# Routed experts: three more parts of rows do their second layer with the rows moving, and the buffer for turned results is doubled

## The chip, the cores and the metric

One core of a Trainium2 chip runs the whole kernel as one program. TensorE (PE, with PEld for its loading of the stationary operand), VectorE (DVE), ScalarE (ACT), GpSimd (POOL) and SyncE (SP) each work through their own list of instructions and wait for each other by semaphores. The metric is the device time in microseconds (us); the median of three runs counts.

## The reference, cut to what matters

```
# x: (8, 1856, 256) -> rfft over 1856, complex 256x256 layer, soft threshold, irfft -> 14848 rows of 256
for each row:  group g = argmax(x @ w_group), expert e = argmax(x @ w_expert[g]), weight = g_w * e_w
for each of the 16 experts:  h = relu(rows @ w1[e])     # 256 -> 1024, the first layer
                             out[rows] = weight * (h @ w2[e])   # 1024 -> 256, the second layer
```

Each row goes to one expert. The sizes of the experts' groups of rows depend on the data, so the kernel sorts rows into lists in memory and works through fixed portions of these lists; a loop at the end takes what is left over.

## The kernel before, in words

**Two stages.** The first 440 us or so are the transform, the routing, and early portions of four experts, in an order written out by hand (the string ORDER). The change leaves this stage alone. Then comes the loop over **parts** (`for i, (kind, q) in enumerate(jobs)`): 40 parts of 256 to 432 rows, each of one expert. Their rows are, in the order of the work (part 0 first):

```
0-3    256 304 432 400        15-17  256 384 336       27-29  256 384 256
4-6    384 384 336            18-20  256 384 288       30-32  256 320 256
7-8    256 256                21-23  256 384 288       33-35  256 320 256
9-11   384 384 320            24-26  256 384 256       36-37  416 384
12-14  384 384 288                                     38-39  320 384
```

**A step.** Step i of the loop issues, in this order on every engine: the second layer of part i-1 (wholly or in part), the first layer of part i, the preparing of the rows of part i+1, and what was left of the second layer of part i-1. The order of instructions on each engine is the order of this code; no scheduler moves them.

**First layer** (`up_g`). The hidden units come in 8 blocks of 128. For a block TensorE runs 6 matmuls with the part's rows moving (line 619; values are split into a high and a low half, so three products per half of the 256 inputs). ScalarE then takes the block out of PSUM with a ReLU (line 624, high half `hh`), and VectorE makes the low half `hl` (line 627). Between the blocks other work is issued: after odd blocks a piece of `back_g` (below), after even blocks a piece of `deal_g`, which gathers rows for part i+2 by indirect DMA on POOL (line 560) and passes them on by SP (line 572). In steps where weights of a coming expert arrive, 8 pieces of weight splitting stand between the blocks as well (line 524 on ScalarE, 525 on VectorE).

**Second layer, plain** (`down_g`). For each tile of up to 128 rows: 16 matmuls, the rows' hidden values as the stationary operand and 512 or 256 columns of weights moving (lines 695 and 696). A last tile of 48 or 80 rows has the same 16 matmuls. ScalarE and VectorE each take out one half (lines 700 and 701), and POOL stores the tile's rows in the output by an indirect DMA (line 669). Two tiles are done before the first layer of part i, the remaining tiles after it.

**Second layer, turned** (`turned_g`, `back_g`). 48 matmuls with the weights stationary and all rows of the part moving (line 717), all before the first layer of part i. The result has the 256 outputs on the partitions, in two halves; ScalarE and VectorE copy one each into the tile `yt` (line 719). In the *next* step, inside the first layer of part i+1, TensorE turns `yt` back with two transposes for each tile of rows (line 730), two tiles after block 1 and the rest after block 3; ScalarE and VectorE scale them out (lines 738 and 736), and POOL stores them. Nothing is left for after the first layer.

**Which parts are turned** (line 1446): those whose row count is in TURNED and whose predecessor is not turned: parts 1, 3, 11, 14, 20, 23, 31, 34, 36 and 38, ten in all.

Preparing the rows of part i+1 (`turn_rows`, lines 582 to 589) takes VectorE and ScalarE; TensorE needs the result at the next first layer. Where the second layer of part i-1 leaves tiles for after the first layer, these matmuls give ScalarE and VectorE time to take out the last blocks before the second layer of part i reads them.

Of the kernel before, what the change touches and what calls it, by code (L numbers as in the profile page):

```python
# [9 lines left out]
F32 = mybir.dt.float32  # L10
# [27 lines left out]
CUTS = ((384, 384, 336), (384, 384, 320), (384, 384, 288), (256, 384, 336), (256, 384, 288), (256, 384, 288), (256, 384, 256),  # L38
        (256, 384, 256), (256, 320, 256), (256, 320, 256), (416, 384), (320, 384))
FCUTS = ((256, 256), (432,), (400,), (256, 304))  # L40
TURNED = (400, 416, 320, 304, 288)
WIDE = 432
LAM = 0.01

# [92 lines left out]
def spectral_moe(ctx: ExitStack, tc: tile.TileContext, x, wri, bri, wgate, w1, w1q, w2, cst, out):  # L137
# [304 lines left out]
    def drain(gen):  # L442
        for _ in gen:
            pass
# [85 lines left out]
    def emit(todo, n):  # L530
        for _ in range(min(n, len(todo))):
            piece, i, cs = todo.pop(0)
            piece(i, cs)

    def fetch(mp, ids, bufs, rows=NPAD + 1, late=False):
        n = ids.n
        out_ = []
        for c0 in range(0, n, 2):
            w = min(2, n - c0)
            xg = mp.tile([128, 2, D], F32, name="xg", bufs=bufs)  # L540
            for c in range(w):
                m = ids.rows(c0 + c)
                ins = nc.gpsimd.indirect_dma_start(
                    out=xg[0:m, c, :], out_offset=None, in_=ys_d[0:rows, :],
                    in_offset=bass.IndirectOffsetOnAxis(ap=ids.gi[0:m, c0 + c:c0 + c + 1], axis=0))
                if late:
                    behind(ins, "stores of the early jobs go first")
            out_.append((xg, w, ids.rows(c0 + w - 1)))
        return out_
# [109 lines left out]
    def h_tiles():  # L659
        return hq.tile([128, 8, WIDE], F32R, name="hh"), hq.tile([128, 8, WIDE], F32R, name="hl")  # L660
# [15 lines left out]
    def down_g(pp, nm, h2, ids, wt, key, tiles, end=False):  # L676
        hh, hl = h2
        w2b, w2h = wt[2], wt[3]
        for t in tiles:
            m = ids.rows(t)  # L680
            o = pp.tile([128, 512], F32, name=nm)[0:m]
            ts = slice(t * 128, t * 128 + m)
            gate_w = ids.ent[0:m, t, 1:2]
            ysb = yp[-1].tile([128, D], F32, name="yo")[0:m]
            if end and t == ids.n - 1:
                o = o[:, 0:D]
                for f in range(8):
                    for a_, b_ in ((hh, w2h), (hh, w2b[:, 1]), (hl, w2h)):
                        nc.tensor.matmul(o, lhsT=a_[:, f, ts], rhs=b_[:, f, :], start=f == 0 and a_ is hh and b_ is w2h,
                                         stop=f == 7 and a_ is hl)  # L690
                nc.scalar.activation(out=ysb, in_=o, func=AF.Copy, scale=gate_w)
                store(ysb, ids, t, key)
                return
            for f in range(8):
                nc.tensor.matmul(o, lhsT=hh[:, f, ts], rhs=w2b[:, :, f, :], start=f == 0, stop=f == 7, skip_group_check=True)  # L695
                nc.tensor.matmul(o[:, 0:D], lhsT=hl[:, f, ts], rhs=w2h[:, f, :], start=False, stop=f == 7,  # L696
                                 skip_group_check=True)
                if f == 3:
                    yield
            nc.scalar.activation(out=ysb, in_=o[:, D:], func=AF.Copy, scale=gate_w)  # L700
            nc.vector.scalar_tensor_tensor(out=ysb, in0=o[:, 0:D], scalar=gate_w, in1=ysb, op0=ALU.mult, op1=ALU.add)  # L701
            store(ysb, ids, t, key)
            yield

    def down(*args):
        drain(down_g(*args))

    def turned_g(pp, nm, h2, ids, wt, yt):
        hh, hl = h2
        w2b, w2h = wt[2], wt[3]  # L710
        n = ids.rows()
        for dh in range(2):
            o = pp.tile([128, 512], F32, name=nm)[:, 0:n]
            ds_ = slice(dh * 128, dh * 128 + 128)
            for f in range(8):
                for w_, h_ in ((w2h, hh), (w2h, hl), (w2b[:, 1], hh)):
                    nc.tensor.matmul(o, lhsT=w_[:, f, ds_], rhs=h_[:, f, 0:n], start=f == 0 and h_ is hh and w_ is w2h,  # L717
                                     stop=f == 7 and h_ is hh and w_ is not w2h)
            (nc.vector.tensor_copy if dh else nc.scalar.copy)(out=yt[:, dh, 0:n], in_=o)
            yield  # L720

    def back_g(pp, nm, yt, ids, key):
        for t0 in range(0, ids.n, 2):
            o = pp.tile([128, 512], F32, name=nm)
            tiles = range(t0, min(ids.n, t0 + 2))
            for t in tiles:
                m = ids.rows(t)
                for dh in range(2):
                    c = (t - t0) * 256 + dh * 128
                    nc.tensor.transpose(o[0:m, c:c + 128], yt[:, dh, t * 128:t * 128 + m], ident)  # L730
            for t in tiles:
                m, cs = ids.rows(t), slice((t - t0) * 256, (t - t0) * 256 + 256)
                ysb = yp[-1].tile([128, D], F32, name="yo")[0:m]
                gate_w = ids.ent[0:m, t, 1:2]
                if t % 2:
                    nc.vector.tensor_scalar(out=ysb, in0=o[0:m, cs], scalar1=gate_w, scalar2=None, op0=ALU.mult)
                else:
                    nc.scalar.activation(out=ysb, in_=o[0:m, cs], func=AF.Copy, scale=gate_w)
                store(ysb, ids, t, key)
            yield  # L740
# [3 lines left out]
    jobs = [(0, 0), (0, 1), (1, 0), (1, 1), (0, 2), (1, 2), (2, NF), (3, NF)]  # L744
# [417 lines left out]
    xq = ctx.enter_context(tc.tile_pool(name="xq", bufs=2, reuse_waits="tile"))  # L1162
# [253 lines left out]
    def of(k):  # L1416
        return [("r", (k, i)) for i in range(len(CUTS[k]))]

    def fixed(e):
        return [("l", (e, i)) for i in range(len(FCUTS[e]))]  # L1420

    jobs = fixed(3) + fixed(1) + fixed(2) + of(0) + fixed(0)
# [4 lines left out]
    raws, jids, jw, rids, ready = {}, {}, {}, {}, {}  # L1427
# [18 lines left out]
            jids[j] = fids[q[0]][1][q[1]]  # L1446

    def turned(i):
        return 0 < i < len(jobs) - 1 and jids[i].rows() in TURNED and not turned(i - 1)

    prev, behind_, todo, ahead = None, iter(()), [], {}
    DEALT = jobs.index(("r", (0, 0)))
# [6 lines left out]
    for i, (kind, q) in enumerate(jobs):  # L1459
        ids = jids[i]  # L1460
        if kind == "r":
            wt = wts["r", q[0]] = jw[i] if i in jw else wts["r", q[0]]
        else:
            wt = wts[q[0]] = jw[i] if i in jw else wts[q[0]]
        nxt = fetch(xp2, jids[i + 1], 3, late=i == 0) if i + 1 < DEALT else None
        rest, back = iter(()), behind_
        behind_ = iter(())
        if prev is not None:
            pids = prev[1]
            if turned(i - 1):  # L1470
                yt = xq.tile([128, 2, WIDE], F32, name="yt", bufs=1)
                rest = turned_g(psy, "py", prev[0], pids, prev[2], yt)
                drain(rest)
                behind_ = back_g(psy, "py", yt, pids, "out")
            else:
                n2 = min(2, pids.n)
                down(psy, "py", prev[0], pids, prev[2], "out", range(n2))
                rest = down_g(psy, "py", prev[0], pids, prev[2], "out", range(n2, pids.n))
        ready.pop(i, lambda: None)()
        gathers = iter(())  # L1480
        if DEALT <= i + 2 < len(jobs):
            if jobs[i + 2][0] == "r":
                k, part = jobs[i + 2][1]
                jids[i + 2] = rids[k][part]
            ahead[i + 2] = []
            gathers = deal_g(jids[i + 2], ahead[i + 2])
        every = 1 if todo or ids.rows() < 384 else 0
        if i in split_at:
            jw[split_at[i]], todo = split_w(raws.pop(split_at[i]))
        hs = h_tiles()  # L1490
        for f, _ in enumerate(up_g(psh, x2, ids.rows(), wt, hs)):
            if f % 2:
                next(back, None)
            else:
                next(gathers, None)
            if f % 2 or not every:
                emit(todo, 1)
            for _ in range(1 if i else 3):
                next(table, None)
        if i not in split_at or not every:  # L1500
            emit(todo, len(todo))
        if i == 0 or i in split_at:
            dma_next(i)
        if nxt is None and i + 1 < len(jobs):
            x2 = turn_rows(ahead.pop(i + 1).pop(), jids[i + 1])
        drain(gathers)
        drain(rest)
        prev = (hs, ids, wt)
        if nxt is not None:
            x2 = prep(xq, nxt, jids[i + 1].rows())  # L1510
# [66 lines left out]
```

## Time and profile before

| | |
|---|---|
| median of three runs | 1068.2 us (1068.2, 1059.08, 1074.6) |
| the profiled execution | 1074.4 us |
| its span, first to last instruction | 1072.6 us |
| mean granted TensorE clock | 0.986 of full |
| busy share: TensorE, VectorE, ScalarE, POOL | 96%, 69%, 45%, 40% |
| loop over the parts | from 442.6 us to the end |

The profiled execution took 1.8 us more than its span, and lies near the top of the three timed runs. A busy share is an average over both stages. Matmuls overlap, so the time from one matmul's start to the next one's start is what it costs, and the duration in its row is longer than that.

### The profile page before, as it was taken

How to read it: one execution, taken by the hardware profiler on the slowest of the kernel's cores; microseconds unless marked ns; L12 is line 12 of the kernel's file. 1: busy time of each engine (PE TensorE's matmuls, PEld its weight loads, DVE VectorE, ACT ScalarE, POOL GpSimd, SP SyncE). 2: the span in 40 equal slices, each digit the busy share in tenths (PEclk: the TensorE clock that was granted, in tenths of full speed). 3: DMA queues.
4: the chain of work that ended last, by engine and by line, in shares of the span. 5: the costliest groups of instructions: out<-in, count | busy, mean ns of one | idle time of the engine just before them, and what ended most of it. 6: DMA issues, size and time to landing. Idle time of an engine off the chain costs nothing.

```text
span 1072.6 us, 25269 instructions
## 1 busy us (share of the span) xinstructions
PE 1024.9 (96%) x9496; PEld 888.0 (83%) x9496; DVE 742.3 (69%) x1754; ACT 484.4 (45%) x1273; POOL 434.0 (40%) x600
## 2 busy tenths in 40 slices
PE   8999999999999999999999999999999999999996
PEld 4886767776867888889988899979998898999995
DVE  6879999999998665436566665665665656767652
ACT  2664645545636243234344444444544535445532
POOL 0120164465463657633235324334342343443432
PEclk9999999999999999989999999999998999999998
DMA  9402512412314320312342442433424244244210
GB/s 383 146 2 91 187 42 106 152 63 81 121 60 180 122 105 28 126 53 67 126 139 79 142 140 72 137 88 126 146 68 135 62 146 140 70 143 139 79 52 29
DMA packets 63407, 117.25 MB, mean 109 GB/s; under 512 B 20588, under 2 KB 44473, under 8 KB 56754
## 3 DMA queue, kind: packets, MB, share of 16 engines
q1 hardware_dynamic: 46450, 67.81, 19.7%
q0 software_dynamic: 11936, 30.79, 9.0%
q10 hardware_dynamic: 4896, 17.01, 4.1%
q8 instruction: 76, 1.25, 0.5%
q14 instruction: 49, 0.40, 0.1%
HBM read 71.37 MB, written 32.46 MB: 97 GB/s over the span
## 4 chain that ended last, share of the span: by engine, by line
PE 61%; DVE 17%; issue 8%; POOL 4%; DMA 3%; SPq 3%; ACT 2%; another core or an unknown queue 0%; ACTq 0%; POOLq 0%; DVEq 0%
PE ph L619 20%; PE py L695 8%; PE pw L887 5%; PE py L717 5%; PE py L696 4%; SPq L572 3%; PE ph L1047 2%; PE pw L869 2%; PE bank L805 2%; PE bank L911 2%; PE bank L929 2%; DVE big L525 2%; DVE hl L627 2%; PE bank L435 2%; DVE big L439 2%
## 5 line engine op out<-in xcount | busy, mean ns | idle before, releaser
L619 PE MATMUL ph<-xth,big 128*128 128x256 f32 (+8 forms) x1280 | 291.7, 312 | 3.8 <-ACT xth L588 3.0
L627 DVE SCALAR_TENSOR_TENSOR hl<-ph,hh 128x256 fp32r<-128x256 f32 (+8 forms) x528 | 167.6, 355 | 132.6 <-ACT hh L624 78.4
L624 ACT ACTIVATE hh<-ph 128x256 fp32r<-128x256 f32 (+8 forms) x528 | 151.2, 339 | 182.1 <-PE ph L619 134.0
L695 PE MATMUL py<-big,hh 128*128 128x512 f32 (+2 forms) x608 | 222.5, 404 | 1.9 <-ACT hh L624 1.4
L619 PEld LDWEIGHTS ph<-xth,big 128*128 128x128 f32 x1280 | 216.6, 188 | 7.6 <-ACT xth L588 5.0
L619 PE MATMUL ph<-xtl,big 128*128 128x256 f32 (+8 forms) x640 | 199.1, 311 | 2.8 <-DVE xtl L589 2.4
L669 POOL DMA_INDIRECT out_dram<-yo,si_r x92 | 92.6, 1006 | 251.0 <-DVE yo L701 204.7
L696 PE MATMUL py<-big,hl 128*128 128x256 f32 (+2 forms) x608 | 175.5, 289 | 5.2 <-DVE hl L627 4.8
L695 PEld LDWEIGHTS py<-big,hh 128*128 128x128 f32 (+2 forms) x608 | 115.7, 190 | 30.3 <-ACT hh L624 2.3
L560 POOL DMA_INDIRECT xg<-ys_d,gi_r x92 | 93.7, 1018 | 89.7 <-ACT hh L624 60.5
L696 PEld LDWEIGHTS py<-big,hl 128*128 128x128 f32 (+2 forms) x608 | 116.0, 191 | 10.4 <-DVE hl L627 10.1
L619 PEld LDWEIGHTS ph<-xtl,big 128*128 128x128 f32 x640 | 120.4, 188 | 5.1 <-DVE xtl L589 4.3
L717 PE MATMUL py<-hh,big 128*128 128x320 f32 (+4 forms) x320 | 75.2, 319 | 1.4 <-DVE yo L701 1.2
L588 ACT CAST xth<-xtf 128x512 fp32r<-128x512 f32 (+5 forms) x59 | 28.4, 518 | 106.6 <-DVE xtf L582 106.6
L582 DVE STREAM_TRANSPOSE xtf<-xm 64x384 f32<-64x384 f32 (+3 forms) x144 | 72.9, 506 | 3.4 <-DMA xm<-xg 2.0
L525 DVE TENSOR_TENSOR big<-xt,big 128x512 fp32r<-128x512 f32 x104 | 71.0, 682 | 5.7 <-ACT big L524 4.4
L853 POOL TENSOR_TENSOR xdl<-xd,xdh 128x512 fp32r<-128x512 f32 (+1 forms) x23 | 28.0, 1217 | 107.4 <-ACT xdh L846 87.1
L887 PE MATMUL pw<-wh,xh 128*128 128x256 f32 x240 | 66.6, 300 | 2.8 <-DVE pw L877 2.8
L524 ACT CAST big<-xt 128x512 fp32r<-128x512 f32 x104 | 65.4, 629 | 0.0
L892 ACT ACTIVATE big<-pw,nlam 128x512 f32<-128x512 f32 x60 | 41.3, 689 | 46.4 <-PE pw L887 45.5
L887 PE MATMUL pw<-wl,xh 128*128 128x256 f32 x240 | 62.0, 280 | 0.0
L887 PEld LDWEIGHTS pw<-wh,xh 128*128 128x128 f32 x240 | 45.1, 188 | 16.9 <-DVE pw L877 7.5
(263 smaller groups left out, 2004.1 us busy)
## 6 DMA issues: line engine op xcount, KB each, us to landing
xt<-in_w_dram SPq DMA_DIRECT2D x21, 1024.0 KB
ys_d<-ysb ACTq DMA_DIRECT2D x32, 512.0 KB
xt<-in_w1q_dram SPq DMA_DIRECT2D x13, 1024.0 KB
xm<-xg SPq DMA_DIRECT2D x290, 32.0 KB
big<-in_x_dram SPq DMA_DIRECT2D x8, 1024.0 KB
xt<-in_x_dram SPq DMA_DIRECT2D x8, 1024.0 KB
xm<-xg SPq DMA_DIRECT2D x144, 16.0 KB
xg<-ys_d,gi_r POOLq DMA_INDIRECT x92
```

Of the source, the lines that this page charges most:

```text
L524: nc.scalar.copy(out=wt[:, 2 * i, cs], in_=raws[i][:, cs])
L525: nc.vector.tensor_tensor(out=wt[:, 2 * i + 1, cs], in0=raws[i][:, cs], in1=wt[:, 2 * i, cs].bitcast(F32), op=ALU.subtract)
L560: ins = nc.gpsimd.indirect_dma_start(out=xg[0:m, c, :], out_offset=None, in_=ys_d[0:NPAD + 1, :], in_offset=bass.IndirectOffsetOnAxis(ap=i ...
L582: nc.vector.transpose(out=xt[64 * to:64 * to + 64, :, 0:k, 32 * a_:32 * a_ + 32].rearrange("f b c t -> f c b t"), in_=xm[64 * a_:64 * a_ + ...
L619: nc.tensor.matmul(o[:, :n], lhsT=a_[:, ch, fs], rhs=b_[:, ch, 0:n], start=k == 0, stop=k == 5)
L624: ins = nc.scalar.activation(out=hh[:, f, cs], in_=o[:, cs], func=AF.Relu)
L627: nc.vector.scalar_tensor_tensor(out=hl[:, f, cs], in0=o[:, cs], scalar=0.0, in1=hh[:, f, cs].bitcast(F32), op0=ALU.max, op1=ALU.subtract)
L669: ins = nc.gpsimd.indirect_dma_start(out=out, out_offset=bass.IndirectOffsetOnAxis(ap=ids.si[0:ids.rows(t), t:t + 1], axis=0), in_=ysb, in ...
L695: nc.tensor.matmul(o, lhsT=hh[:, f, ts], rhs=w2b[:, :, f, :], start=f == 0, stop=f == 7, skip_group_check=True)
L696: nc.tensor.matmul(o[:, 0:D], lhsT=hl[:, f, ts], rhs=w2h[:, f, :], start=False, stop=f == 7, skip_group_check=True)
L717: nc.tensor.matmul(o, lhsT=w_[:, f, ds_], rhs=h_[:, f, 0:n], start=f == 0 and h_ is hh and w_ is w2h, stop=f == 7 and h_ is hh and w_ is n ...
L887: ins = nc.tensor.matmul(y, lhsT=a_[:, h, k % 2, j], rhs=t[:, j, h], start=False, stop=a_ is xl and h == 1, skip_group_check=True)
```

## The change

The list TURNED gains 432 and 336, the rule that a turned part's predecessor must not be turned is dropped, and `yt` gets the pool's two buffers in place of one.

```diff
-TURNED = (400, 416, 320, 304, 288)
+TURNED = (432, 400, 416, 336, 320, 304, 288)
...
     def turned(i):
-        return 0 < i < len(jobs) - 1 and jids[i].rows() in TURNED and not turned(i - 1)
+        return 0 < i < len(jobs) - 1 and jids[i].rows() in TURNED
...
             if turned(i - 1):
-                yt = xq.tile([128, 2, WIDE], F32, name="yt", bufs=1)
+                yt = xq.tile([128, 2, WIDE], F32, name="yt")
                 rest = turned_g(psy, "py", prev[0], pids, prev[2], yt)
                 drain(rest)
                 behind_ = back_g(psy, "py", yt, pids, "out")
```

Three parts become turned: part 2 (432 rows, four tiles, between the turned parts 1 and 3), part 6 (336 rows, three tiles) and part 17 (336 rows, three tiles). Thirteen are then turned.

On ScalarE at the end of step 3 and in step 4, the order of instructions (minus: before, plus: changed) reads as follows; `ent_f_177` belongs to part 2, and the copy of 400 columns is that of part 3:

```order
 L588 CAST xth<-xtf 128x2x256
 L588 CAST xth<-xtf 128x2x128
-L700 ACTIVATE yo<-py,ent_f_177 128x256
-L700 ACTIVATE yo<-py,ent_f_177 48x256
 L719 COPY yt<-py 128x400
 L624 ACTIVATE hh<-ph 128x256
```

The two tiles of part 2 that stood after the first layer of part 3 are gone from there; they are taken out inside the first layer of part 4 instead.

On POOL, steps 18 to 20 before the change read as follows; `si_r_8572` are stores of part 17, `si_r_9184` stores of parts 18 and 19, `gi_r_9183` and `gi_r_9781` gathers for parts 20 and 21:

```order
L669 DMA out_dram<-yo,si_r_8572 16384x256 x3
L354 CAST gi_r_9781<-ent_r_9780 128x8
L356 TENSOR_SCALAR ixt<-ent_r_9780 128x8
L357 TENSOR_SCALAR ixt<-ixt 128x8
L358 TENSOR_TENSOR ixt<-ixt,ent_r_9780 128x8
L359 CAST si_r_9782<-ixt 128x8
L560 DMA xg<-ys_d,gi_r_9183 128x256 x2
L560 DMA xg<-ys_d,gi_r_9183 32x256
L669 DMA out_dram<-yo,si_r_8572 16384x256
L669 DMA out_dram<-yo,si_r_9184 16384x256 x2
L560 DMA xg<-ys_d,gi_r_9781 128x256 x2
L669 DMA out_dram<-yo,si_r_9184 16384x256 x2
```

The same stretch after the change (the stores of part 17 are now `si_r_8570`, those of part 18 and 19 `si_r_9182`, the gathers for parts 20 and 21 `gi_r_9181` and `gi_r_9779`):

```order
L560 DMA xg<-ys_d,gi_r_9181 128x256 x2
L560 DMA xg<-ys_d,gi_r_9181 32x256
L669 DMA out_dram<-yo,si_r_9182 16384x256 x2
L560 DMA xg<-ys_d,gi_r_9779 128x256
L669 DMA out_dram<-yo,si_r_8570 16384x256 x2
L560 DMA xg<-ys_d,gi_r_9779 128x256
L669 DMA out_dram<-yo,si_r_8570 16384x256
L669 DMA out_dram<-yo,si_r_9182 16384x256 x2
```

Part 17's three stores have moved from before and after the first layer of part 18 into the first layer of part 19, between two gathers; with the two stores of part 18 ahead of them, that first layer has seven indirect DMAs where it had five with one of them earlier.

## Rows read from the trace of the kernel before

**Rows 1.** The page: busy time of TensorE, its share and its instructions.

```profile
PE 1024.9 (96%) x9496; PEld 888.0 (83%) x9496; DVE 742.3 (69%) x1754; ACT 484.4 (45%) x1273; POOL 434.0 (40%) x600
```

**Rows 2.** Stretch: length; busy (instructions) of PE, PEld, DVE, ACT, POOL; clock, DMA.

```profile
442.62:1072.60 629.98, 602.69 (x3732) 559.00 (x3732) 381.25 (x1012) 272.13 (x804) 240.22 (x304) 0.98 0.35 105
```

**Rows 3.** Stretches: first layer of 432, its two pairs of tiles, part 3 turned, 336.

```profile
475.77:485.19 9.42, 9.42 (x50) 8.98 (x49) 5.40 (x21) 4.15 (x14) 2.01 (x2) 1.00 0.11 31
486.16:491.91 5.75, 5.75 (x34) 5.03 (x33) 2.05 (x6) 1.08 (x3) 1.98 (x2) 1.00 0.24 57
501.33:506.93 5.60, 5.60 (x34) 4.37 (x32) 3.32 (x12) 3.02 (x9) 1.31 (x2) 1.00 0.29 74
506.93:517.17 10.24, 9.05 (x50) 8.71 (x49) 5.28 (x13) 2.03 (x5) 1.91 (x2) 1.00 0.44 136
724.74:732.16 7.42, 7.42 (x51) 7.42 (x49) 3.59 (x12) 3.54 (x14) 3.96 (x4) 1.00 0.68 246
732.16:740.61 8.45, 8.45 (x51) 7.37 (x50) 4.78 (x14) 2.19 (x7) 2.97 (x3) 1.00 0.27 67
```

**Rows 4.** TensorE in order of time: start, us, engine, line, operation [idle before, releaser].

```profile
494.10 0.60 PE L730 MATMUL py<-K,yt 128*128 128x128 f32 x4
494.46 0.43 PE L619 MATMUL ph<-xth,big 128*128 128x400 f32 x1
...
496.73 0.38 PE L730 MATMUL py<-K,yt 128*48 128x128 f32 x2
496.86 0.43 PE L619 MATMUL ph<-xth,big 128*128 128x400 f32 x1
```

**Rows 5.** Groups on TensorE from 442.62 us: line, shape, count, busy us, mean ns.

```profile
L730 PE MATMUL py<-K,yt 128*128 128x128 f32 (+4 forms) x64 | 10.1, 272 | 0.0
```

**Rows 6.** Waits on TensorE, 506.93 to 517.17: us in total, times, longest.

```profile
PE py L717 <- DVE yo L701: 1.2, 1, 1.2
```

**Rows 7.** Stretches: second layers of parts 16, 22 and 25 after turned parts' transposes.

```profile
714.18:724.74 10.56, 8.51 (x33) 6.20 (x33) 8.56 (x22) 5.95 (x17) 1.03 (x2) 0.84 0.39 115
...
805.02:816.60 11.58, 9.90 (x34) 7.12 (x33) 8.28 (x20) 5.07 (x15) 1.08 (x2) 0.71 0.45 137
852.36:862.07 9.71, 8.31 (x34) 6.16 (x34) 7.37 (x18) 4.93 (x14) 0.42 (x2) 0.82 0.32 85
```

**Rows 8.** POOL in step 16, in order of time: first and last of six.

```profile
705.87 1.04 POOL L669 DMA_INDIRECT out_dram<-yo,si_r  x1 [6.88 <-DVE yo L701]
...
712.44 0.98 POOL L560 DMA_INDIRECT xg<-ys_d,gi_r  x1 [0.31 <-issue]
```

**Rows 9.** TensorE in step 16, the last matmul of block 3.

```profile
709.63 0.34 PE L619 MATMUL ph<-xth,big 128*128 128x384 f32 x1
```

**Rows 10.** ScalarE in step 16: blocks 2, 3 and 4 taken out.

```profile
710.37 0.55 ACT L624 ACTIVATE hh<-ph 128x256 fp32r<-128x256 f32 x2 [1.47 <-PE py L730]
...
713.28 0.55 ACT L624 ACTIVATE hh<-ph 128x256 fp32r<-128x256 f32 x2 [1.85 <-PE ph L619]
...
715.58 0.52 ACT L624 ACTIVATE hh<-ph 128x256 fp32r<-128x256 f32 x2
```

**Rows 11.** Stretches: first and second layer of part 19, first layer of part 20.

```profile
754.69:763.01 8.32, 8.32 (x51) 8.32 (x49) 6.92 (x19) 7.50 (x22) 3.16 (x3) 1.00 0.25 74
763.01:768.65 5.64, 5.64 (x33) 4.92 (x33) 4.86 (x12) 2.27 (x7) 0.00 (x0) 1.00 0.22 47
768.65:775.50 6.85, 6.61 (x50) 6.39 (x49) 3.87 (x14) 2.97 (x12) 4.48 (x5) 1.00 0.96 341
```

**Rows 12.** Stretches: second layers of parts 8 and 33; part 36 turned.

```profile
587.53:595.01 7.48, 6.36 (x35) 4.78 (x33) 5.68 (x15) 3.15 (x9) 0.94 (x1) 1.00 0.73 239
...
959.70:965.32 5.62, 5.62 (x35) 4.91 (x33) 3.60 (x8) 1.20 (x3) 3.86 (x4) 1.00 0.37 112
...
1002.12:1012.14 10.02, 9.61 (x49) 8.91 (x49) 5.58 (x12) 2.57 (x7) 2.87 (x3) 1.00 0.28 71
```

## The prediction, made before the changed kernel was run

> **What bounds the kernel now.** I read the page first, then TensorE by stretches, then its waits, then single instructions. On the page TensorE is busy for 96% of the span and VectorE, the next, for 69% [rows 1]. The change touches only the loop over the parts, so its stage counts: from 442.62 us to the end TensorE is busy for 602.69 of 629.98 us at a mean clock of 0.98 [rows 2]. Only 27.3 us are idle there. TensorE is therefore the bound, and the change has to be priced in TensorE's time: columns that it no longer moves, transposes that it has to add, and waits that go or come. Removed or added work on ScalarE, VectorE and POOL counts only where TensorE comes to wait for it.
>
> The stretches give the price of matmuls. A first layer of 432 rows is 48 matmuls and takes 9.42 us; one of 336 rows takes 7.42 us [rows 3]. That is 9.42/48/432 = 0.454 and 7.42/48/336 = 0.460 ns for a column, so the time follows the rows moved. A plain second layer doesn't follow them: part 2 takes 5.75 us for two full tiles and 5.60 us for a full tile and one of 48 rows; part 6 takes 8.45 us for three tiles, the last of 80 rows [rows 3]. A tile costs 2.8 us however few its rows.
>
> **The change, part by part.**
>
> *Second layers.* A turned one is 48 matmuls over all rows, as the first layer is. Part 2: 9.42 for 5.75 + 5.60 = 11.35 us, -1.93. Parts 6 and 17: 7.42 for 8.45 us, -1.03 each. Together **-3.99 us**.
>
> *Transposes.* Two for each tile: 8 for part 2, 6 each for parts 6 and 17, 20 in all. In the trace four of them hold TensorE for 0.36 us (494.10 to 494.46) and two for 0.13 us (496.73 to 496.86), though each has a mean duration of 0.272 us [rows 4, 5]: they overlap. Part 2 costs 2 x 0.36 and the other two 0.36 + 0.13 each: 0.72 + 0.98 = **+1.70 us**.
>
> If they did not overlap they would cost 20 x 0.272 = 5.44 us. The Trainium skill, "TensorE: Matmul & The Clock Gate", section "Part 4: PE-mode transpose", gives about 275 ns for one in a kernel, mostly latency of the memory access, and adds that it does not count as busy for the clock gate; by that price the term would be an estimated 20 x 0.275 = 5.5 us. The trace speaks against it here: the starts above leave 0.09 us for each.
>
> *The wait of part 3.* Its turned second layer took 10.24 us, while 9.42 x 400/432 = 8.72 is its price [rows 3]. 1.2 us of that is one wait for a PSUM buffer that VectorE still had to empty of a tile of part 2 [rows 6]. These tiles no longer stand there: **-1.52 us**. What is late next is the first-layer blocks of part 3, since nothing lies between the first layer and the second any more. The only like case is part 36, turned right after a first layer that carries back transposes: 10.02 us against 9.42 x 416/432 = 9.07 [rows 12], 0.95 more. Bounds 0 and +0.95; I take **+0.95**, as the structure is the same.
>
> *The back work inside the next first layers.* This decides the sign. Step 16 shows what such a layer can do. POOL issues six indirect DMAs one after another, the first at 705.87 and the last ending at 713.42 [rows 8]. In that time ScalarE falls behind: block 3's last matmul ends at 709.63 + 0.34 = 709.97, but ScalarE takes the block out at 713.28, after a wait of 1.85 us that is put down to that very matmul, and block 4 at 715.58 [rows 9, 10]. So it came 3.3 us after its data, while POOL was still issuing. I can't see the mechanism, only that the two go together. The second layer of the same part begins at 714.18 and reads these blocks in order; it took 10.56 us, and its likes in parts 22 and 25 took 11.58 and 9.71, at clocks of 0.84, 0.71 and 0.82 [rows 7], against 5.64 us for part 19 at 1.00 [rows 11]. The loss was 4.92, 5.94 and 4.07 us, mean 4.98. Those three are the plain second layers that follow a first layer with back transposes and weight splitting, with no rest tile between.
>
> Part 17's back work moves into just such a layer, that of part 19: seven indirect DMAs, eight pieces of weight splitting, no rest tile after it. ScalarE, busy for 7.50 of 8.32 us there [rows 11], gets two scale-outs more. Bounds 4.07 and 5.94; I take the mean, 4.98. Against it, the first layer of part 20 has 0.57 us of waiting today (6.85 against 9.42 x 288/432 = 6.28) [rows 11], which the longer stretch before it would hide. Net **+4.41 us**, net bounds 3.50 and 5.37.
>
> Part 6's back work moves into the first layer of part 8, 5.64 us long by its rows, with four pieces of splitting and no rest tile after it. Its second layer already takes 7.48 us, 1.84 over [rows 12]. Bounds: nothing more, and the worst of the three stalls, 11.58 - 7.48 = +4.10. Half the splitting of step 19 puts it near the middle: **+2.0 us**.
>
> Part 2's back work moves into the first layer of part 4, without splitting; part 4's second layer follows directly. Part 33's, after a layer with back transposes and few splitting pieces, took 5.62 us, no loss [rows 12]. Bounds 0 and part 8's 1.84; I take the middle, **+0.9 us**.
>
> *Cover that shrinks.* The rest tiles of parts 6 and 17 also gave time for preparing the rows of parts 8 and 19. Now the two tiles of parts 7 and 18 alone do, 5.64 us. Part 20's first layer, with that cover today, lost 0.57 us, so 0 to 0.57 each; I take 0, since the added turned layers don't lengthen the preparing. The second `yt` buffer moves addresses and nothing on a queue: 0. The moved stores go on ending long before the next step's; POOL is busy for 240 of 630 us [rows 2].
>
> **Sum**: -3.99 + 1.70 - 1.52 = -3.81 us for TensorE's own work and the old wait; +0.95 + 0.9 + 2.0 + 4.41 = +8.26 us for new waits; **+4.45 us**. The profiled execution took 1074.4 us, so its like would take 1078.9. That execution lies 6.2 us above the median, and timed runs go by the median: 1068.2 + 4.45 = 1072.65, **1073 us**. The bounds: without new waits 1064.4; with each wait at its upper end (0.95 + 1.84 + 4.10 + 5.37 = 12.26, and 1.14 for the cover) 1077.8.
>
> **Rivals.**
>
> *The saving shows (chance 0.24, 1064.4 us).* ScalarE keeps up, or its lag comes from something else in steps 16, 22 and 25 than the POOL run and the back work together, and no new wait appears. For it: part 33, and part 8's layer has few rows to take out. Against: three of three layers like that of part 19 stalled. Only the -3.81 us is left.
>
> *Slower by waits at three places (chance 0.15, 1081.3 us).* ScalarE falls behind in the first layers of parts 4, 8 and 19 alike, and each following second layer stalls until the clock drops as in part 22. Price: 0.95 + 5.94 + 4.10 + 5.94 = 16.93 over -3.81, +13.1 us. It decides as soon as part 4 and part 8 stall as part 22 did; without these the forecast holds. For it: the clock of 0.71 in such a stretch. Against: part 4 has no splitting beside it, and part 33 had no loss.
>
> *Transposes at their whole duration (chance 0.04, 1076.4 us).* 5.44 for 1.70, +3.74 us on the forecast. The starts above speak against it.
>
> That the change does not do what it says is out: the new order shows the three parts turned, thirteen in all, and their rest tiles gone.
>
> **How the numbers follow.** The forecast keeps 0.57. Its own range, with the bounds, is about 1068 to 1078, and the medians of so few runs move: the three shown lie between 1059.08 and 1074.6. The range takes in the saving of 1064.4 with 4 us for that below it, and the slow rival with 2 us above it: **1060 to 1083**. What a measurement of this kernel can tell from no change is about 2%, 21 us. No case reaches it: even the slow rival with the whole transposes is +17. So within 2% has 0.93, faster by more 0.02 and slower by more 0.05, the last for a stall at several places that spreads to the steps behind.
>
> **What would show it.** Right: part 2's second layer as 48 matmuls in about 9.4 us, those of parts 6 and 17 in 7.4; part 3's turned layer near 9.7 without the wait for VectorE; ScalarE taking blocks of parts 19 and 8 out microseconds after their last matmul, beside POOL's run of stores and gathers; part 19's second layer near 10.6 us at a clock below 1, part 8's near 9.5. Wrong: part 19's second layer still at 5.6 us (then the saving shows); part 4's above 8 (then the slow rival); the matmul behind four transposes a microsecond later; or a difference in the first 440 us, which the change leaves alone.

## The result, and the profile after

The changed kernel takes 1073.82 us (median of 20 runs, 1066.87 to 1081.38), the kernel before 1068.05 us (median of 20, 1059.08 to 1074.6). The ratio is **1.0055, with a 95% interval of 1.0035 to 1.0075**: 5.9 us slower (3.7 to 8.0). The forecast was 1073 us, 4.45 us slower.

The page's line on TensorE answers to [rows 1]; the span is 1073.2 us, 0.6 us above that of before.

```profile
PE 1025.5 (96%) x9500; PEld 891.5 (83%) x9500; DVE 741.4 (69%) x1751; ACT 484.9 (45%) x1272; POOL 431.7 (40%) x600
```

Two profiled executions that differ by 0.6 us can't show 5.9 us as a whole (that of before lies 6.2 us above its median, that of after 1.2). They can be laid beside each other part by part, since TensorE does the parts in one order. These are the stretches of the changed kernel that answer to [rows 3, 7, 11, 12]; columns as in [rows 2]. In order: second layer of part 2; of part 3; first and second layer of part 4; second layer of part 6; first and second layer of part 8; of part 19; first layer of part 20.

```profile
484.95:494.54 9.59, 9.59 (x50) 9.14 (x49) 1.56 (x5) 1.12 (x3) 0.94 (x1) 1.00 0.19 43
503.95:512.71 8.76, 8.76 (x49) 8.69 (x49) 6.20 (x16) 3.37 (x9) 0.34 (x1) 1.00 0.24 54
512.71:521.90 9.19, 9.19 (x58) 9.11 (x57) 4.90 (x18) 3.60 (x12) 5.45 (x6) 1.00 0.68 236
521.90:530.04 8.14, 7.06 (x33) 4.84 (x33) 4.47 (x14) 2.53 (x9) 1.39 (x2) 1.00 0.41 126
559.52:566.92 7.40, 7.40 (x51) 7.40 (x49) 2.41 (x5) 1.44 (x3) 2.19 (x6) 1.00 0.22 53
578.78:585.17 6.39, 6.39 (x57) 6.38 (x55) 3.73 (x12) 2.61 (x6) 4.47 (x5) 1.00 0.34 92
585.17:596.46 11.29, 7.98 (x35) 6.03 (x33) 6.77 (x19) 4.58 (x12) 3.83 (x4) 0.85 0.63 205
753.83:762.95 9.12, 9.12 (x57) 9.03 (x56) 5.89 (x15) 5.40 (x16) 6.80 (x7) 1.00 0.31 94
762.95:772.30 9.35, 8.45 (x33) 6.26 (x33) 7.73 (x19) 5.16 (x15) 0.34 (x1) 0.82 0.33 81
772.30:778.65 6.35, 6.35 (x50) 6.35 (x49) 3.09 (x11) 2.84 (x11) 4.88 (x5) 1.00 0.94 355
```

Of the kernel before, first and second layer of part 4 and first layer of part 8:

```profile
517.17:525.49 8.32, 8.32 (x50) 8.32 (x49) 4.97 (x20) 3.87 (x14) 2.88 (x3) 1.00 0.46 175
525.49:531.14 5.65, 5.65 (x34) 4.92 (x33) 4.57 (x13) 1.85 (x5) 0.00 (x0) 1.00 0.24 50
581.89:587.53 5.64, 5.64 (x50) 5.64 (x49) 3.89 (x13) 3.19 (x8) 3.48 (x3) 1.00 0.39 107
```

The turned second layers have the lengths of their columns: 9.59 us for part 2, where 5.75 and 5.60 stood, and 7.40 for part 6, where three plain tiles took 8.45 [rows 3]. Part 3 follows at once in 8.76 us, where 10.24 stood. And the three plain second layers behind the new transposes are stretched: 8.14, 11.29 and 9.35 us against 5.65, 7.48 and 5.64 before, at clocks of 1.00, 0.85 and 0.82.

Why is seen beside part 19. POOL works through seven indirect DMAs, 1.3 us apart; the first, the fourth and the last two:

```profile
754.33 1.03 POOL L669 DMA_INDIRECT out_dram<-yo,si_r  x1 [6.50 <-DVE yo L701]
...
758.26 1.10 POOL L669 DMA_INDIRECT out_dram<-yo,si_r  x1 [0.30 <-issue]
...
760.97 0.99 POOL L560 DMA_INDIRECT xg<-ys_d,gi_r  x1 [0.30 <-issue]
762.26 1.03 POOL L669 DMA_INDIRECT out_dram<-yo,si_r  x1 [0.30 <-issue]
```

TensorE's last matmul of block 4 is the first of the two in this row (the other begins block 5); it ends at about 759.59 + 0.34 = 759.93:

```profile
759.59 0.52 PE L619 MATMUL ph<-xth,big 128*128 128x384 f32 x2
```

ScalarE takes block 3 out at 759.52, and block 4 only at 762.93, 3.0 us after its data, though it stood idle for 1.19 us just before; the other rows are a scale-out and a piece of splitting:

```profile
759.52 0.57 ACT L624 ACTIVATE hh<-ph 128x256 fp32r<-128x256 f32 x2
760.76 0.47 ACT L738 ACTIVATE yo<-py,ent_r 80x256 f32<-80x256 f32 x1 [0.67 <-issue]
761.13 0.61 ACT L524 CAST big<-xt 128x512 fp32r<-128x512 f32 x1
762.93 0.55 ACT L624 ACTIVATE hh<-ph 128x256 fp32r<-128x256 f32 x2 [1.19 <-PE ph L619]
764.40 0.55 ACT L624 ACTIVATE hh<-ph 128x256 fp32r<-128x256 f32 x2 [0.41 <-PE py L695]
```

The second layer of part 19 began at 762.95 and had to wait for blocks 4 to 7. The packed trace also has the times at which TensorE's semaphore was raised, and they tell which side is late. The last matmuls of blocks 4 to 7 end at about 759.93, 760.99, 762.05 and 763.11. After 759.31 no raise is recorded until 762.91, then come 764.38, 764.46, 764.53 and more in quick order. ScalarE takes out block 4 0.02 us after the first of these and block 5 0.02 us after the second. So the signal itself came late, and ScalarE started as soon as it was there.

One measure of this is used below: the blocks, out of the 320 first-layer blocks of the loop, that ScalarE took out more than 0.4 us after their last matmul though it was idle for as long. There are 52 before and 61 after.

One thing the forecast had not: VectorE, in order of time, at the start of part 0. Before:

```profile
442.48 0.07 DVE L1333 MEMSET ones_f<- 128x16 f32 x1
442.65 0.69 DVE L607 TENSOR_TENSOR xtl<-ph,xth 128x512 fp32r<-128x512 f32 x1
```

After:

```profile
444.56 0.07 DVE L1333 MEMSET ones_f<- 128x16 f32 x1 [2.84 <-DMA out_dram<-yo,si_b]
444.73 0.69 DVE L607 TENSOR_TENSOR xtl<-ph,xth 128x512 fp32r<-128x512 f32 x1
```

A memset of 0.07 us waits 2.84 us for a store of the first stage: the second `yt` moves the addresses of everything allocated after it, and `ones_f` now lies where rows wait to be stored. `xtl` is queued behind it, and TensorE needs `xtl`; before, and after:

```profile
443.39 0.39 PE L619 MATMUL ph<-xtl,big 128*128 128x256 f32 x1 [0.39 <-DVE xtl L607]
...
445.48 0.58 PE L619 MATMUL ph<-xtl,big 128*128 128x256 f32 x1 [3.28 <-DVE xtl L607]
```

The first layers of parts 0 and 1 and the second layer of part 1, before:

```profile
442.62:449.82 7.20, 6.81 (x54) 6.38 (x55) 5.53 (x24) 3.04 (x9) 5.59 (x11) 1.00 0.23 65
455.57:466.81 11.24, 8.73 (x59) 7.64 (x57) 4.56 (x22) 4.52 (x18) 6.77 (x7) 0.91 0.32 96
466.81:475.77 8.96, 8.96 (x49) 8.96 (x49) 1.66 (x6) 0.86 (x2) 2.02 (x6) 0.73 0.07 18
```

and after:

```profile
441.81:454.25 12.44, 9.16 (x54) 8.74 (x54) 6.84 (x29) 3.08 (x8) 9.31 (x23) 0.73 0.19 50
459.99:467.71 7.72, 7.72 (x58) 7.50 (x56) 4.97 (x23) 4.57 (x18) 3.38 (x4) 1.00 0.26 76
467.71:474.54 6.83, 6.83 (x51) 6.83 (x50) 1.38 (x5) 0.99 (x3) 2.96 (x7) 1.00 0.09 24
```

Part 0 lost 5.24 us: 2.89 of longer waiting, and 2.35 of more busy time (9.16 for 6.81) at a clock of 0.73. Part 1 gained 3.52 + 2.13 = 5.65 us: here the new wait only took the place of an old one. The old one goes with POOL again: before, POOL works off eight indirect DMAs in a row there, from 453.11 to 463.10; after, the longer part 0 has split them, with 2.46 us of idle time between the first four and the next.

From the first layer of part 2 to that of part 21, the region of the change, the changed kernel lost 4.40 us against the other; the forecast said 4.45, and what that agreement is worth is said below. Outside it the two executions differ by what looks like chance: part 22's second layer was 3.00 us shorter after, part 25's 3.66 shorter, part 36's turned one 3.07 longer, though the change touches none of them.

### The profile page after: what moved, and what is told of

It reads as the page before. It is cut to its first block, busy times and chain, and to the rows that moved or that the text cites. A ratio compares the mean times of both kernels' runs of the same rounds, so it can differ in the third digit from the quotient of the medians.

```text
span 1073.2 us, 25253 instructions
## 1 busy us (share of the span) xinstructions
PE 1025.5 (96%) x9500; PEld 891.5 (83%) x9500; DVE 741.4 (69%) x1751; ACT 484.9 (45%) x1272; POOL 431.7 (40%) x600
## 4 chain that ended last, share of the span: by engine, by line
PE 58%; DVE 16%; issue 10%; POOL 6%; DMA 4%; ACT 3%; SPq 2%; another core or an unknown queue 1%; POOLq 0%; ACTq 0%; DVEq 0%
PE ph L619 20%; PE py L717 8%; PE py L695 6%; PE pw L887 5%; PE py L696 3%; PE pw L869 2%; PE bank L929 2%; PE bank L911 2%; DMA big<-in_x_dram 2%; PE bank L805 2%; DVE xtf L582 2%; POOL out_dram L669 2%; PE ph L1047 2%; PE bank L961 2%; SPq L572 2%
## 5 line engine op out<-in xcount | busy, mean ns | idle before, releaser
L619 PE MATMUL ph<-xth,big 128*128 128x256 f32 (+8 forms) x1280 | 295.7, 314 | 1.6 <-ACT xth L588 0.9
L619 PEld LDWEIGHTS ph<-xth,big 128*128 128x128 f32 x1280 | 218.9, 190 | 6.0 <-ACT xth L588 3.7
L695 PE MATMUL py<-big,hh 128*128 128x512 f32 x528 | 193.6, 404 | 4.5 <-ACT hh L624 4.0
L696 PE MATMUL py<-big,hl 128*128 128x256 f32 x528 | 152.7, 289 | 4.2 <-DVE hl L627 3.3
L695 PEld LDWEIGHTS py<-big,hh 128*128 128x128 f32 x528 | 101.3, 192 | 28.6 <-ACT hh L624 4.9
L696 PEld LDWEIGHTS py<-big,hl 128*128 128x128 f32 x528 | 101.5, 192 | 9.9 <-DVE hl L627 8.4
L717 PE MATMUL py<-hh,big 128*128 128x320 f32 (+6 forms) x416 | 98.5, 320 | 1.7 <-ACT hh L624 1.7
L717 PEld LDWEIGHTS py<-hh,big 128*128 128x128 f32 x416 | 72.3, 190 | 2.9 <-ACT hh L624 2.1
L717 PE MATMUL py<-hl,big 128*128 128x320 f32 (+6 forms) x208 | 66.8, 321 | 0.6 <-DVE hl L627 0.6
```

What stands on the lines that cost most here:

```text
L619: nc.tensor.matmul(o[:, :n], lhsT=a_[:, ch, fs], rhs=b_[:, ch, 0:n], start=k == 0, stop=k == 5)
```

## The experiments

**Theory A** is the forecast's: while POOL works off indirect DMAs back to back, TensorE's signals reach ScalarE and VectorE late, and a second layer with no rest tiles before it pays. **Theory B**, its rival: the scale-outs and the weight splitting are too much for ScalarE and VectorE. **Theory C**: the address of the second `yt` buffer costs time by itself. The twelve runs fell on three chips, and these differ: the kernel before took 1044.05 us on the first, 1072.70 on the second and 1043.02 on the third. Each kernel is compared with the kernel before on its own chip. All runs on a chip were made in one sitting, so where this text says chip, it could be the sitting as well.

### First chip: one part of the change at a time

*only_432*: of the three parts only part 2 is turned.

```diff
-TURNED = (432, 400, 416, 336, 320, 304, 288)
+TURNED = (432, 400, 416, 320, 304, 288)
```

Expected: 

> Only part 2 (432 rows) is added to the turned parts; parts 6 and 17 stay plain. By the terms of the prediction: -1.93 (second layer) +0.72 (transposes) -1.52 (wait of part 3) +0.95 +0.9 = -0.9 us. By the trace of the change, from the second layer of part 2 to the first layer of part 6: -0.8 us. Both theories: 1067 us, no difference that can be measured. If part 2 alone made the change slower: 1072 or more.

Measured: 1047.01 against 1044.05 us, ratio 1.0027 (1.0006 to 1.0049). Slower by 3.0 us, where both theories said 0.8 faster.

*only_336*: only parts 6 and 17 are turned.

```diff
-TURNED = (432, 400, 416, 336, 320, 304, 288)
+TURNED = (400, 416, 336, 320, 304, 288)
```

Expected: 

> Only parts 6 and 17 (336 rows each) are added to the turned parts; part 2 stays plain. By the terms of the prediction: -2.06 +0.98 +2.0 +4.41 = +5.3 us. By the trace of the change, from the first layer of part 6 to that of part 21: +5.2 us. Expected: 1073 us, with part 8's second layer above 9 us and part 19's above 9 us. If the slowing comes from somewhere else: 1067 us or less.

Measured: 1046.15 us, ratio 1.0015 (0.9995 to 1.0035), and the stalls that it should have shown are not there. First and second layer of part 19 in this kernel:

```profile
738.40:747.44 9.04, 9.04 (x56) 8.95 (x55) 7.63 (x20) 8.13 (x24) 7.07 (x7) 1.00 0.29 88
747.44:753.07 5.63, 5.63 (x33) 4.91 (x33) 4.85 (x12) 2.40 (x7) 0.33 (x1) 1.00 0.25 62
```

POOL has the same seven DMAs with the same 0.3 us between them; two of them, with TensorE's end of block 4 and ScalarE's taking it out:

```profile
742.68 1.25 POOL L669 DMA_INDIRECT out_dram<-yo,si_r  x1 [0.30 <-ACT hh L624]
744.23 0.99 POOL L669 DMA_INDIRECT out_dram<-yo,si_r  x1 [0.30 <-DVE big L525]
```

```profile
744.14 0.51 PE L619 MATMUL ph<-xth,big 128*128 128x384 f32 x2
```

```profile
744.55 0.56 ACT L624 ACTIVATE hh<-ph 128x256 fp32r<-128x256 f32 x2
```

Block 4 ends at 744.14 + 0.34 = 744.48 and is taken out at 744.55, 0.07 us later; in the changed kernel above it was 3.0 us. The raises of TensorE's semaphore stand 0.01 to 0.02 us behind the ends of its matmuls here. ScalarE is busier here (8.13 of 9.04 us, against 5.40 of 9.12 above) and yet in time. That speaks against Theory B. On this chip 0 of 320 blocks are late, in each of the four kernels run on it.

*late_stores*: the changed kernel, with the stores of turned results held back.

```diff
...
 # back_g
-                store(ysb, ids, t, key)
+                held.append((ysb, ids, t, key))
...
 # after the eight blocks of a first layer
+        release(step_end[-1])    # stores what is held; each waits for the last hh
```

Expected: 

> The changed kernel, but the stores of all turned results are issued on POOL only when ScalarE has taken out the last block of the first layer; transposes and scale-outs stay where they are. Theory A, the run of indirect DMAs on POOL makes TensorE's signals late for ScalarE and VectorE: the second layers of parts 4, 8 and 19 go from 8.14, 11.29 and 9.35 us to near 5.7 (part 8 to 7.5 or less), and those of parts 16, 22, 25 lose their stalls as well: 1056 to 1064 us. Theory B, the scale-outs and the weight splitting overload ScalarE and VectorE: the stalls stay, 1072 to 1075 us.

Measured: 1046.82 us, ratio 1.0025 (1.0000 to 1.0051). Neither number came: no second layer was stalled here to begin with, so holding the stores back had nothing to win.

*burst_alone*: the run on POOL without any turning.

```diff
-            store(ysb, ids, t, key)
+            if ids is HOLD[0]:        # parts 6, 17, 25, 28
+                held.append((ysb, ids, t, key))
+            else:
+                store(ysb, ids, t, key)
...
+                if i - 2 in (6, 17, 25, 28) and f in (1, 3):
+                    for _ in range(2 if f == 1 else 1):
+                        store(*held.pop(0))
...
```

Expected: 

> The kernel before, nothing turned in addition, but the three stores each of parts 6, 17, 25 and 28 are held back on POOL and issued where a turned part's stores would be: two after block 1 and one after block 3 of the first layer of parts 8, 19, 27 and 30 (seven buffers for stored rows in place of four, so that nothing waits for a buffer). Theory A, the run of indirect DMAs alone does it: the second layers of parts 8 and 19 take 8 to 11 us in place of 7.48 and 5.64, those of parts 27 and 30 (5.62, 5.61) up to 8; in all 3 to 10 us slower, 1071 to 1078 us. Theory B, scale-outs and transposes are what makes ScalarE late: 1067 to 1069 us, and these second layers as before.

Measured: 1041.86 us, ratio 0.9978 (0.9962 to 0.9993). The longer runs cost nothing on this chip: second layers of 5.60 and 5.64 us for parts 8 and 19. So **a run of DMAs on POOL is not enough by itself** on such a chip. Whether it would be where signals are late this run can't say; the count below does. That the kernel came out 2.2 us faster than before is not explained; it has seven buffers for stored rows in place of four.

What slowed the other three on this chip is part 0. Its first layer in *only_432*, and in *burst_alone*, which has one `yt` buffer:

```profile
438.24:450.67 12.43, 9.15 (x55) 8.72 (x55) 6.83 (x29) 3.16 (x9) 9.31 (x23) 0.73 0.20 50
```

```profile
440.07:447.28 7.21, 6.81 (x54) 6.39 (x55) 5.53 (x24) 3.16 (x9) 5.59 (x11) 1.00 0.23 66
```

Here the wait of the memset costs 5.2 us, and part 1 has nothing to give back: its first layer takes 7.71 us with one buffer as with two. From the first layer of part 2 to that of part 6, *only_432* is 1.0 us shorter than *burst_alone*, which still has part 2 as before: 5.2 - 1.0 = 4.2 us slower, within the interval of 0.6 to 5.1.

### Second chip: signals late again

*yt_only* is the kernel before with two `yt` buffers:

```diff
-                yt = xq.tile([128, 2, WIDE], F32, name="yt", bufs=1)
+                yt = xq.tile([128, 2, WIDE], F32, name="yt")
```

Expected: 

> The kernel before with the second yt buffer alone; nothing more is turned. Theory C, the buffer moves the addresses of what is allocated after it, so that VectorE's small memset of line 1333 lands where rows of the first stage are still being stored, waits 2.8 us for that store, and TensorE waits 3.3 us in the first layer of part 0 and drops its clock: part 0's first layer takes 12.4 us in place of 7.2, and the kernel is 3 to 6 us slower than before. Theory of the prediction (the buffer costs 0): within 1 us of before.

*as_changed* is the changed kernel. Expected: 

> The changed kernel itself, to have it on the same chip as the others. By what the single parts measured there: +5.2 us (part 0) -1.0 us (part 2 turned) -1.2 us (parts 6 and 17 turned) = +3.0 us against before, if signals to ScalarE are not late on this chip; +5.8 us as in the result if they are late again.

*yt_apart* is the changed kernel with the second buffer behind all others:

```diff
+    yts = [xq, ctx.enter_context(tc.tile_pool(name="yq", bufs=1, reuse_waits="tile"))]
...
-                yt = xq.tile([128, 2, WIDE], F32, name="yt")
+                yts.reverse()
+                yt = yts[0].tile([128, 2, WIDE], F32, name="yt", bufs=1)
```

Expected: 

> The changed kernel, but the second yt buffer has a pool of its own behind all others, so that no other tile changes its address. Theory C: the first layer of part 0 takes 7.2 us again and the kernel is 5 us faster than the changed one: -2.2 us against before where signals are not late, about +1 us where they are. If the buffer's place costs nothing: as the changed kernel, +3 to +6 us.

*yt_apart_late* has that and the late stores. Expected: 

> As the kernel with the buffer apart, and the stores of turned results are issued only when ScalarE has taken out the last block of the first layer. Theory A, a run of indirect DMAs on POOL makes TensorE's signals late: where they are late, the second layers of parts 4, 8, 19 (and 16, 22, 25) are back near 5.7 us and the kernel is 8 to 15 us faster than before; where they are not late, the stores' place changes nothing and the time is that of the kernel with the buffer apart, within 1.5 us.

Measured, the kernel before at 1072.70 us (two of the four expectations missed outright: *yt_only* was to be 3 to 6 us slower by Theory C and was not, and *yt_apart* was to be about 1 us slower and was 8.0):

| kernel | us | ratio to before | late blocks of 320 |
|---|---|---|---|
| yt_only | 1072.44 | 0.9995 (0.9965 to 1.0025) | 53 |
| as_changed | 1080.85 | 1.0083 (1.0056 to 1.0111) | 53 |
| yt_apart | 1080.73 | 1.0080 (1.0052 to 1.0108) | 58 |
| yt_apart_late | 1057.27 | 0.9856 (0.9822 to 0.9889) | 42 |

On this chip Theory C falls: with the buffer apart part 0 is back at 7.21 us, but part 1 then takes 11.22 and 8.78 us, and the sum is the same, as in the result. The late stores are worth 23.5 us over the same kernel without them. Second layers of parts 4, 8 and 19 in *yt_apart*:

```profile
524.26:533.56 9.30, 8.45 (x34) 6.23 (x33) 5.53 (x16) 2.85 (x9) 1.37 (x2) 0.82 0.23 55
588.26:599.68 11.42, 8.70 (x35) 6.04 (x33) 6.61 (x19) 4.46 (x12) 3.73 (x4) 0.85 0.61 208
767.40:776.57 9.17, 7.09 (x33) 4.81 (x32) 7.17 (x18) 5.60 (x17) 0.95 (x1) 1.00 0.30 65
```

and in *yt_apart_late*:

```profile
524.75:530.40 5.65, 5.65 (x33) 4.92 (x33) 4.51 (x13) 1.85 (x5) 3.70 (x4) 1.00 0.42 116
583.96:592.95 8.99, 7.08 (x34) 4.82 (x33) 6.60 (x19) 4.35 (x12) 4.33 (x4) 1.00 0.71 229
754.69:761.11 6.42, 6.04 (x34) 4.79 (x33) 5.64 (x15) 3.06 (x10) 3.36 (x3) 1.00 0.31 83
```

The transposes, the scale-outs and the splitting stand in the first layers as before; only the stores have left them. Parts 16, 22 and 25 lost their stalls with it (9.65, 10.77 and 8.08 us became 6.52, 5.81 and 6.17). Part 8 kept much of its stall (8.99 us) and 42 blocks are still late, so not all of these layers went back to near 5.7 us, as had been expected; what remains goes with the two stores of the plain second layer and the gathers, which still make runs on POOL.

The kept traces tell A from B once more. For each of the 1920 blocks of the six executions with late signals (before, after, and the four above), count how many indirect DMAs POOL had begun in one run, under 0.6 us apart, when the block's last matmul ended; a run that ended more than 2.5 us earlier counts as none.

| DMAs in the run | blocks | late |
|---|---|---|
| none or one | 703 | 0 |
| two | 430 | 60 |
| three or more | 787 | 259 |

In first layers with neither transposes nor splitting, 127 of 388 blocks behind three or more are late; in those with splitting, 123 of 387. Where POOL had begun at most one and the DMA engines were over half busy in the 3 us before, none of 92 is. **That decides for Theory A against B where signals are late**: lateness goes with the run and not with the work of ScalarE and VectorE, nor with DMA traffic as such.

### Third chip: signals in time

Three of four kernels tell what the change is worth without new waits; the fourth was meant for a chip with late signals. *before_late* is the kernel before with the edit of *late_stores*. Expected: 

> The kernel before (ten turned parts, one yt buffer), with the stores of turned results issued only when ScalarE has taken out the last block of the first layer. Theory A (runs of indirect DMAs on POOL make TensorE's signals late): on a chip where they are late, the second layers of parts 16, 22 and 25 fall from 9.7 to 11.6 us to below 7, and the kernel is 8 to 13 us faster than before; on a chip where they are not, within 1.5 us of before. Theory B (scale-outs and splitting overload ScalarE): as before on either.

*yt_apart_late_2* is *yt_apart_late* again. Expected: 

> The same kernel as the one with the buffer apart and the stores late, beside the kernel before with late stores. With the new waits gone, what is left of the change is TensorE's own saving: -3.99 + 1.70 = -2.3 us against the kernel before with late stores, and up to -3.8 us with the wait of part 3. If turning the three parts costs something besides the stores: no faster than the kernel before with late stores.

*all_late* turns parts 6 and 17 alone and holds more stores:

```diff
...
-            store(ysb, ids, t, key)
+            if key and t < 2 and not end:
+                held.append((ysb, ids, t, key))
+            else:
+                store(ysb, ids, t, key)
```

Expected: 

> Parts 6 and 17 turned in addition (part 2 plain, one yt buffer), seven buffers for stored rows in place of four, and all stores that would be issued during a first layer, also the two of the plain second layer, are held until ScalarE has taken out its last block. Only gathers are left beside the first layers. Theory A: where signals are late, second layers of parts 8, 16, 19, 22, 25 near 5.7 us and 2 to 5 us faster than the kernel with only the turned stores late; where they are not late, 1 to 2 us faster than before. Rival: a run of five or more stores at once beside the second layers makes these wait instead, and nothing is won over the kernel with turned stores late.

*no_stores* is the changed kernel without the stores of the loop's parts, so its output lacks their rows:

```diff
...
     def store(ysb, ids, t, key):
+        if in_loop:
+            return
```

Expected: 

> The changed kernel without the stores of the loop's parts: their output rows are left out. POOL's indirect DMAs in the loop are then the gathers alone. Theory A: where signals are late, the second layers of parts 4, 8, 16, 19, 22 and 25 take 5.6 to 6.5 us, as with late stores, and the time is at or below that of the kernel with the buffer apart and late stores plus the 5 us of part 0. Theory B, scale-outs and splitting on ScalarE and VectorE: these second layers stay at 8 to 11 us.

Measured, the kernel before at 1043.02 us, 0 of 320 blocks late in all four:

| kernel | us | ratio to before |
|---|---|---|
| before_late | 1042.58 | 0.9994 (0.9976 to 1.0012) |
| yt_apart_late_2 | 1038.55 | 0.9956 (0.9943 to 0.9969) |
| all_late | 1040.95 | 0.9981 (0.9969 to 0.9993) |
| no_stores | 1037.37 | 0.9956 (0.9940 to 0.9973) |

Late stores alone change nothing here, as Theory A has it for such a chip. With the three parts turned, the kernel is 4.0 us faster than with late stores alone. In the traces the loop is 3.0 us shorter (the spans differ by 0.3 us only, since the first stage, the same in both, took 2.6 us longer). 1.0 us of it lies between parts 2 and 6, 1.1 between the second layers of parts 6 and 7, and 1.0 between those of parts 17 and 18, less 1.4 for parts 8 and 19, which have new transposes, and the parts after them: 1.7 us are the change's own in this pair of traces. Another 1.6 us is a wait in part 10 that came and went in other kernels too. All second layers of parts 4, 8, 16, 19, 22 and 25 took 5.6 to 5.7 us; that of part 19 in *yt_apart_late_2*:

```profile
744.46:750.12 5.66, 5.66 (x34) 4.92 (x33) 4.88 (x13) 2.40 (x7) 3.11 (x3) 1.00 0.42 107
```

*no_stores* can't tell A from B here, since nothing was late. Whether all stores held back would win more where signals are late stays open.

## Why the prediction was right

The forecast was 4.45 us slower, and 5.9 (3.7 to 8.0) was measured; the mechanism that set the sign is the one the traces show. Step by step, [rows 3, 7, 11, 12] against the rows above:

- *Second layers* (-3.99): part 2 takes 9.59 for 11.35 us, parts 6 and 17 7.40 each for 8.45. That is -1.76 - 2.10 = **-3.86**. Right, though the row of 8.45 us is not what it was read as: it is the rest tile of part 16 and the first two tiles of part 17, all of 128 rows. The tile of 80 rows comes later, and with the two tiles of part 18 it took 8.44 us, so the price holds.
- *Transposes* (+1.70): the first layers of parts 4, 8 and 19 grew by 0.87, 0.75 and 0.80 us, **+2.42**, or 0.12 us for each of the 20 rather than 0.09. They overlap, as [rows 4] said; the rival with their whole duration falls. By the 275 ns that the Trainium skill gives for one ("TensorE: Matmul & The Clock Gate", "Part 4: PE-mode transpose") it would have been an estimated 5.5 us; the trace does not agree.
- *Wait of part 3* (-1.52 + 0.95): it took 8.76 us, 0.04 over its price, so **-1.48**. The +0.95 from part 36 didn't come in this execution (on the second chip 10.06 us did).
- *Part 4* (+0.9, bound 1.84): **+2.49**. The term that was mis-sized most for its size, and the one outside its bounds on the high side: I had taken splitting beside the first layer as needed for a stall, and POOL's run was enough. 8.14 us is the sign that was named for the slow rival; its price of 5.94 did not follow.
- *Part 8* (+2.0, bound 4.10): **+3.81**. Near the bound; half the splitting did not mean half the stall.
- *Part 19* (+4.98, bounds 4.07 to 5.94; -0.57 for part 20): **+3.71** and -0.50. Below the bounds, and right in kind: clock 0.82, ScalarE 3.0 us late.
- *The second `yt` buffer* (0: "moves addresses and nothing on a queue"): **wrong as a step**. It put a wait of 2.84 us on VectorE's queue, 5.2 us for part 0. Where signals were late an old wait of part 1 fell away for it, so the number held by luck; on the first chip it outweighed what turning won.

Measured, these terms of the region come to -3.86 + 2.42 - 1.48 + 2.49 + 3.81 + 3.71 - 0.50 = **+6.59 us**, not +4.45. The region lost only 4.40 because of stretches that have no term in the forecast: part 5's second layer was 1.61 us shorter and part 9's 0.93, part 5's first layer 0.62 longer. So the mechanism and the sign are right, and that the number came out within 1.5 us is in part luck: stalls that were sized too small at parts 4 and 8 met savings that were not foreseen, and the cost of the buffer met the wait of part 1.

What the forecast did not see is that its main term belongs to some chips. All three stalls it leaned on [rows 7] were absent on two of the three chips, with the same order on POOL. The changed kernel as it stands was not timed on those two. There the rival "the saving shows" is right as soon as the buffer lies apart: 0.44% faster than before, with late stores that change nothing by themselves there. **The version that beats both kernels** is the change with the buffer apart and the late stores: 1.44% faster than before on the second chip (interval 1.11 to 1.78%), 0.44% on the third (0.31 to 0.57%). How much of the 1.44% the late stores would give the kernel before by themselves stays open: that kernel with late stores was run on the third chip only.

Open is why signals are late on one chip and not on another. The traces show it only as a pair: late blocks lie beside runs of indirect DMAs, and vanish with the run or with the chip. A rival that no run here tests is the recording itself. Every execution was recorded, the timed ones too (each has its span and clock), and where signals are late the records have holes: of the raises of TensorE's, VectorE's and ScalarE's semaphores in the loop the trace after the change has 639 of 713, 558 of 709 and 520 of 696, that of *only_336* 713 of 719, 708 of 713 and 693 of 705.

## What to carry to other kernels

Before work is moved into a stretch, count what it puts on POOL's queue there, not only on the engines that compute: runs of two or more indirect DMAs made TensorE's hand-over up to microseconds late on some chips, and a consumer without spare work behind it pays. A buffer added in the middle of an allocation is not free: list the new waits that it gives to whatever lies after it, down to a memset of 0.07 us, and put the buffer last. Where a stall may depend on the chip, a forecast should give the time with and without it, and both kernels have to be timed on the same chip.

## What the runs showed of the hardware

The same kernel took 1043 to 1044 us on two chips and 1068 to 1073 us where signals were late. In the traces the difference is not the clock of an undisturbed stretch, which is 1.00 on all: it is 42 to 61 of 320 blocks handed over late, by up to 6.6 us, in six profiled executions of one kind, and none of 320 in eight of the other. Late blocks stood behind two or more indirect DMAs in a row, 319 of 1217, and never behind one or none, 0 of 703 (counted as above). A raise of TensorE's semaphore, recorded 0.01 to 0.02 us after its matmul's end in *only_336*, came about 3 us after it where part 19 stalled.

After a wait of 3.3 us on TensorE in part 0 its clock stood at 0.73 over that first layer: the granted clock fell to the lower of its two levels (1.2 GHz) during the wait and was back at the upper one (2.4 GHz) before the layer's end. It was 1.00 in the next stretch.
